# A fused attention and gated feed-forward kernel: the first block's output by seven products, and sums of the gates' weights on GpSimd

## The chip, the cores and the metric

The kernel runs on one core of a Trainium2 chip. The metric is the device time of one execution in microseconds (us). A core has a matmul engine (TensorE, PE in the profile; its weight loads are PEld), VectorE (DVE), ScalarE (ACT), GpSimd (POOL) and SyncE (SP). They run their own instruction streams and wait for each other by semaphores. Matmul results go to eight PSUM banks of 512 float32 a partition; here they are called pF0 to pF3 and pA0 to pA3.

## The reference

Attention with projected keys and values, then a gated feed-forward layer. There are 8 batches, 8 heads, a sequence of 1024 and a head size of 64; the projection has 64 rows.

```python
def _attn_ref(q, k, v, E, F):
    k_proj = np.einsum('ks,bhsd->bhkd', E, k)
    v_proj = np.einsum('ks,bhsd->bhkd', F, v)
    scale = 1.0 / np.sqrt(q.shape[-1])
    scores = scale * np.matmul(q, k_proj.transpose(0, 1, 3, 2))
    scores = scores - np.max(scores, axis=-1, keepdims=True)
    attn = np.exp(scores)
    attn = attn / (np.sum(attn, axis=-1, keepdims=True) + 1e-09)
    return np.matmul(attn, v_proj).astype(np.float32)

def _moe_ref(x, w_gate, w_val, w_out):        # x: 8192 x 512, d_ff 1536
    gate = 1.0 / (1.0 + np.exp(-(x @ w_gate)))
    val = x @ w_val
    return (gate * val @ w_out).astype(np.float32)
```

The output of attention, with the heads side by side, is `x`.

## The kernel before

The 8192 rows are worked on in 16 blocks of 512, two to a batch. For a block the kernel makes the gates and values (`x @ w_gate`, `x @ w_val`), their product `hT`, and the output `hT @ w_out`. Nearly everywhere a product of two matrices, each cut in 2 x 2 quarters, is made of seven products of quarters instead of eight (Strassen's scheme in Winograd's form). The price is sums of quarters, made beforehand: `xs_sums` of the inputs, `s_sums` of `hT`, and sums of the weights, which are made once: `vt_sums` (values, buffer vT), `gt_sums` (gates, buffer gT) and `t_sums` (output, buffer wT). Two exceptions stand at the start: the gates of blocks 0 and 1 and the values of block 0 are plain products, and so is the output of block 0:

```python
        def oproj(blk, tt, pb, cols=((0, DM),)):
            # ... o is a row of vsnap or ost
            for n, (c0, c1) in enumerate(cols):
                # ...
                for m in range(NF):                        # NF = 12
                    mm(pb, bank[pb][:, 0 : c1 - c0],
                       hT[blk % 2][:, m, tt * P : (tt + 1) * P],
                       wO[:, m, c0:c1], ...)               # 512 columns
                dve(lambda e, pb=pb, c0=c0, c1=c1: e.tensor_scalar(
                        o[:, c0:c1], bank[pb][:, 0 : c1 - c0], 0.5, None, op0=ALU.mult), ...)
                # ... the store of o
```

(Calls are joined to fewer lines in this section, and "..." marks cuts.) A block's output by seven products looks like this; `a` and `c` are two banks, and a product is twelve matmuls of 256 columns:

```python
        def o_chain(blk, a, c, goal, step, sums=True):
            # ...
            if sums:
                for n in (1, 2, 3):
                    s_sums(blk, n, (0, 6))
            prod(a, "A11", "B11", True)
            seed(a, c)                  # ACT copies bank a to bank c
            prod(c, "A12", "B21")
            evac(c, 0, 0)               # ACT, to the output buffer
            s_sums(blk, 4, (0, 6))
            prod(a, "S2", "T2")
            keep_snap(0, a)             # ACT, to a buffer in SBUF
            prod(a, "A21", "T3")
            keep_snap(1, a)
            prod(c, "S1", "T1", True)
            add_snap(1, c, 1, 1)        # DVE, bank c plus the kept one
            prod(a, "A22", "T4")
            evac(a, 1, 0)
            stored(blk, (2, 3))
            prod(c, "A12", "B22")
            add_snap(0, c, 0, 1)
            stored(blk, (0, 1))
```

The sums of the gates' weights; each writes a third or all of one buffer of gT (the one numbered 1 overwrites a part of `wG` itself), and VectorE makes all of them:

```python
        def gt_sums(n, part=None):
            c0, c1 = (0, DFF // 2) if part is None else (256 * part, 256 * part + 256)
            # ... B11 to B22: quarters of wG
            T = [gT[:, k, :, c0:c1] for k in range(3)]
            o, a, b, op = {
                3: (T[1], B22, B12, ALU.subtract),
                1: (B12, B12, B11, ALU.subtract),
                2: (T[0], T[1], B11, ALU.add),
                4: (T[2], B21, T[0], ALU.subtract),
            }[n]
            # ...
            dve(lambda e: e.tensor_tensor(o, a, b, op), r, w, t=0.95 if part is None else 0.42)
```

The first part of the program, up to block 0's output, stands in an order set by hand: `todo` is a list of slots of TensorE's work, and `put` or `on(u, j, ...)` hangs other work on a slot. After the plain gates of block 0 (slots 0 to 10) come three groups of pieces (`u` = 0, 1, 2), the quads K = 3, 4, 5 of block 1, with batch 1's attention among them. Then:

```python
        on(1, 6, lambda: (load_k(2), load_v(2), load_q(2)))       # issued from GpSimd's queue
        # ...
        on(2, 0, h_sums(1, A, 1))
        on(2, 4, h_sums(1, A, 2, 3))
        on(3, 0, h_sums(1, Z, 1, 2, 3))
        for tt in range(4):
            todo.append(lambda tt=tt: oproj(0, tt, FF.take()))
        on(3, 1, n1["outputs"])
        on(3, 2, lambda: n1["bc"](0))     # bc: attention's scaling, two rounds
        on(3, 3, lambda: n1["bc"](1))
```

All that follows is put in order by a list scheduler with times of its own (`arranged`), from `goal`, the wished start. Its first part is, before the change:

```python
        for n in (3, 2):
            t_sums(n)
        for n in (3, 2, 4):
            gt_sums(n)
        gt_sums(1)
        for n in (1, 2, 3, 4):
            xs_sums(2, n)
        next_kv(2, -2.0)                  # projects K and V of batch 2: 16 matmuls
        transpose_q(["kpB"])
        t_sums(4)
        t_sums(1)
        o_chain(1, OA, OC, 0.0, 2.0, sums=False)
        # ... then the chains of quads 6 to 47, with attention among them
```

Every engine takes its own instructions in the order of the program. All loads stand in GpSimd's queue; of those that matter here `second_loads` issues Q, K and V of batch 1 and the two halves of `wO`, the latter once Q of batch 1 has been transposed. The order of `load_w` at the start is that of the pieces of `wG` and `wV`, 256 columns each.

Of the kernel before, what the change touches and what calls it, by code (L numbers as in the profile page):

```python
# [7 lines left out]
ALU = mybir.AluOpType  # L8
# [229 lines left out]
def bass_linformer_attn__then__ffn_glu_sigmoid_kernel(  # L238
# [18 lines left out]
    with contextlib.ExitStack() as es:  # L257
# [33 lines left out]
        bsel8 = within([P, 4, 2, 64], BF16)  # L291
        kp = within([P, NR, DH], BF16)
        rhi = within([P, 256], BF16)
        rhl = within([P, 256], BF16)
        early[0], used[0] = gT[:, :, :, :].rearrange("p a b c -> p (a b c)"), 0
# [176 lines left out]
        def start_loads():  # L472
# [18 lines left out]
            load_w(0, 1)  # L491
            load_w(1)
            load_w(2)
            for R in range(2):
                load_q_half(0, 1, R)
            load_w(3)
            load_w(4)
            load_w(5)
# [456 lines left out]
        def attention(b):  # L955
# [90 lines left out]
            def bc(rnd):  # L1046
                bks = [AA.take() for _ in range(4)]
# [11 lines left out]
                for j in range(4):  # L1059
                    n = 4 * rnd + j  # L1060
                    mul(n // 2, n % 2, bks[j])
                    AA.append(bks[j])
# [230 lines left out]

        def gate(blk, m, pg, pv):
            M = blk * NF + m
# [18 lines left out]
        def oproj(blk, tt, pb, cols=((0, DM),)):  # L1314
            o = vsnap[tt][:, :] if tt < 2 else ost[:, tt, :]
            ok = [("vsnap", tt)] if tt < 2 else None
            t = 2 * (2 * (blk % 2) + tt % 2) + tt // 2
            for n, (c0, c1) in enumerate(cols):
                if n:
                    pb = FF.take()  # L1320
                for m in range(NF):
                    mm(
                        pb,
                        bank[pb][:, 0 : c1 - c0],
                        hT[blk % 2][:, m, tt * P : (tt + 1) * P],
                        wO[:, m, c0:c1],
                        [("hT", blk % 2, m, tt // 2)] + (["wO0", "wO12"] if m < H6 else ["wO1"]),
                        start=(m == 0),
                        stop=(m == NF - 1),
                    )  # L1330
                dve(
                    lambda e, pb=pb, c0=c0, c1=c1: e.tensor_scalar(
                        o[:, c0:c1], bank[pb][:, 0 : c1 - c0], 0.5, None, op0=ALU.mult
                    ),
                    [],
                    ok or [("ost", tt, x) for x in ((0, 1) if len(cols) == 1 else (n,))],
                    b=pb,
                )
                FF.append(pb)
                add(  # L1340
                    "SP",
                    lambda e, c0=c0, c1=c1: e.dma_start(out_v[blk // 2, t][:, c0:c1], o[:, c0:c1]),
                    r=ok or [("ost", tt, x) for x in ((0, 1) if len(cols) == 1 else (n,))],
                    dma=f"out{tt}" if n == 0 else "outlast",
                )

        H6 = NF // 2

        def t_sums(n):
# [6 lines left out]
                4: (T4, B21, T2, ALU.subtract, ["wO1", ("wT", 2)], [("wT", 4)]),  # L1360
                1: (B12, B12, B11, ALU.subtract, ["wO0"], ["wO12", ("wT", 1)]),
            }[n]
            if n == 4:
                w = w + ["bsel8", ("kp", 0), ("kp", 1)]
                w += [(k, R) for k in ("rhi", "rhl") for R in range(2)]
            dve(lambda e: e.tensor_tensor(o, a, b, op), r, w, t=0.95)

        def s_sums(blk, n, ms, eng="DVE"):
# [4 lines left out]
            S1, S2 = hS[:, 0, lo, :], hS[:, 1, lo, :]  # L1373
# [14 lines left out]
        def part(blk, x, up):  # L1388
            if x[0] == "S":
                return [(x, m) for m in up]  # L1390
            return [("hT", blk % 2, m + H6 * (x[2] == "2"), int(x[1]) - 1) for m in up]
# [200 lines left out]
        def gt_sums(n, part=None):  # L1592
# [15 lines left out]
            if n != 1:  # L1608
                w += ["rows", "ident"] + [("rden", c, R) for c in range(2) for R in range(2)]
# [518 lines left out]
```

The softmax here doesn't subtract the row's maximum and nothing guards it: scores larger than these inputs give would overflow.

## Time and profile before

| | |
|---|---|
| time, median of 3 runs | 517.52 us (517.07 to 517.91) |
| span of the profiled execution | 515.9 us |
| TensorE busy | 505.0 us (98%), clock 1.000 |
| VectorE busy | 410.9 us (80%) |
| ScalarE busy | 345.0 us (67%) |
| GpSimd busy | 41.0 us (8%) |
| moved by DMA | 63.13 MB, mean 122 GB/s |

The profile is of one execution. Busy time is the time in which an engine had an instruction at work; the ends of matmuls are modelled, so that a busy TensorE need not be at its peak. VectorE's busy share by stretches of 10 us is 8.0 of 10 us from 60 to 70, 8.8 from 70 to 80, 9.5 from 80 to 90 and 8.4 from 90 to 100; the last two hold the four sums of the gates' weights, 0.95 us each, and the four of the output's weights, 0.95 us each. A line of a timeline has start and time in us, the engine, the line of the kernel, the operation, what it writes and reads, the shape and how many of them; the brackets at the end tell how long the engine sat idle before and what ended it.

### The profile page before, as it was taken

What the parts mean: (1) busy time and instruction counts of PE and PEld (TensorE: products, weight loads), DVE (VectorE), ACT (ScalarE), POOL (GpSimd) and SP (SyncE); (2) the same over time, 40 slices, a digit from 0 to 9 for tenths busy, and PEclk for the clock granted to TensorE, in tenths of its full rate; (3) what the DMA queues carried; (4) which work ended last, traced back from release to release, by engine and by line L of the source; (5) the groups of instructions that cost most, each with busy time, mean ns of one, the idle gap of its engine ahead of it and who ended that gap; (6) DMA issues with size and microseconds to landing.
All of it is one profiled execution on the core that took longest, in us unless ns stands there. A gap on an engine that the chain in (4) does not pass through costs nothing.

```text
span 515.9 us, 11369 instructions
## 1 busy us (share of the span) xinstructions
PE 505.0 (98%) x4598; PEld 410.0 (79%) x4598; DVE 410.9 (80%) x809; ACT 345.0 (67%) x645; POOL 41.0 (8%) x60
## 2 busy tenths in 40 slices
PE   5999999999999999999999999999999999999996
PEld 3545645888888888888888888888888888888885
DVE  4548779899789796988879888797969898777774
ACT  2555683867778677677767776777676766676652
POOL 9420301200200020000100020000000000000000
PEclk9999999999999999999999999999999999999999
DMA  9999999899798788454946389374104330201013
GB/s 161 199 198 204 150 195 221 115 178 233 93 224 155 152 150 138 102 125 123 174 85 154 60 152 203 56 164 100 46 7 97 42 104 1 83 1 76 6 43 124
DMA packets 105205, 63.13 MB, mean 122 GB/s; under 512 B 63040, under 2 KB 97344, under 8 KB 105152
## 3 DMA queue, kind: packets, MB, share of 16 engines
q0 software_dynamic: 34000, 29.89, 37.5%
q1 hardware_dynamic: 71152, 32.52, 28.8%
q8 instruction: 36, 0.59, 0.4%
q14 instruction: 17, 0.14, 0.1%
HBM read 60.29 MB, written 16.78 MB: 149 GB/s over the span
## 4 chain that ended last, share of the span: by engine, by line
PE 94%; DMA 2%; DVE 1%; POOL 1%; issue 0%; ACT 0%; DVEq 0%; POOLq 0%
PE pA L385 51%; PE pF L385 43%; DMA KVs<-in_v_dram 2%; DVE hT L1832 0%; POOL KVs L403 0%; DVE vsnap L1710 0%; POOL Qb L403 0%; DVE xT L868 0%; DVE ost L1437 0%; ACT sig L389 0%; DVE sig L1786 0%; ACT vsnap L389 0%; DVE ost L1522 0%; POOL quad L482 0%; DVE hS L1382 0%
## 5 line engine op out<-in xcount | busy, mean ns | idle before, releaser
L389 ACT ACTIVATE sig<-pA 128x512 f32<-128x512 f32 x126 | 75.1, 596 | 43.4 <-PE pA L385 42.8
L1699 ACT ACTIVATE pF<-pA 128x512 f32<-128x512 f32 x99 | 58.5, 591 | 30.9 <-PE pA L385 26.3
L1710 DVE TENSOR_TENSOR vsnap<-pF,vsnap 128x512 f32<-128x512 f32 x90 | 61.8, 686 | 18.1 <-ACT vsnap L389 9.2
L1786 DVE TENSOR_TENSOR sig<-pF,sig 128x512 f32<-128x512 f32 x84 | 57.5, 685 | 7.2 <-PE pA L385 3.7
L385 PE MATMUL pF<-wO,hT 128*128 128x256 bf16 (+1 forms) x402 | 59.3, 285 | 0.0
L389 ACT ACTIVATE vsnap<-pA 128x512 f32<-128x512 f32 x84 | 50.2, 597 | 11.9 <-PE pA L385 11.8
L1832 DVE SCALAR_TENSOR_TENSOR hT<-sig,vsnap 128x512 bf16<-128x512 f32 x84 | 56.6, 683 | 0.9
L389 ACT ACTIVATE sig<-sig 128x512 f32<-128x512 f32 x84 | 52.8, 629 | 2.9 <-DVE sig L1786 2.6
L385 PE MATMUL pF<-xS,wV 128*128 128x256 bf16 x360 | 54.0, 273 | 0.1
L385 PE MATMUL pA<-xT,gT 128*128 128x256 bf16 x336 | 50.4, 273 | 0.0
L385 PE MATMUL pF<-xS,wG 128*128 128x256 bf16 x336 | 50.4, 273 | 0.0
L385 PE MATMUL pA<-xT,vT 128*128 128x256 bf16 x336 | 50.4, 273 | 0.0
L385 PE MATMUL pF<-xT,wG 128*128 128x256 bf16 (+1 forms) x264 | 50.2, 311 | 0.2 <-DVE xT L868 0.2
L389 ACT ACTIVATE sig<-pF 128x512 f32<-128x512 f32 x66 | 39.5, 598 | 15.0 <-PE pF L385 13.1
L385 PE MATMUL pA<-wT,hT 128*128 128x256 bf16 x360 | 48.8, 273 | 0.1
L1832 DVE SCALAR_TENSOR_TENSOR hT<-sig,pF 128x512 bf16<-128x512 f32 x42 | 28.7, 683 | 24.6 <-PE pF L385 24.4
L385 PEld LDWEIGHTS pF<-wO,hT 128*128 128x128 bf16 x402 | 38.7, 98 | 10.5 <-issue 0.8
L385 PE MATMUL pF<-xT,wV 128*128 128x256 bf16 (+1 forms) x240 | 41.5, 294 | 0.0
L385 PEld LDWEIGHTS pF<-xS,wV 128*128 128x128 bf16 x360 | 34.9, 98 | 6.1 <-DVE vsnap L1710 0.4
L385 PEld LDWEIGHTS pA<-wT,hT 128*128 128x128 bf16 x360 | 34.3, 98 | 5.6 <-ACT EF L389 0.8
L389 ACT ACTIVATE eT<-pA 128x512 bf16<-128x512 f32 x58 | 34.1, 596 | 5.7 <-PE pA L385 4.4
L385 PEld LDWEIGHTS pA<-xT,vT 128*128 128x128 bf16 x336 | 32.3, 98 | 5.2 <-issue 0.4
(159 smaller groups left out, 906.5 us busy)
## 6 DMA issues: line engine op xcount, KB each, us to landing
out_dram<-ost SPq DMA_DIRECT2D x61, 256.0 KB, 2.5
Qb<-in_q_dram POOLq DMA_DIRECT2D x7, 1024.0 KB, 11.9
KVs<-in_k_dram POOLq DMA_DIRECT2D x7, 1024.0 KB, 13.7
KVs<-in_v_dram POOLq DMA_DIRECT2D x7, 1024.0 KB, 18.0
wO<-in_moe_w_out_dram POOLq DMA_DIRECT2D x2, 768.0 KB, 9.8
wG<-in_moe_w_gate_dram POOLq DMA_DIRECT2D x5, 256.0 KB, 18.9
wV<-in_moe_w_val_dram POOLq DMA_DIRECT2D x5, 256.0 KB, 19.4
KVs<-in_k_dram POOLq DMA_DIRECT2D x2, 512.0 KB, 9.3
```

Of the source, the lines that this page charges most:

```text
L385: return add("PE", lambda e: e.matmul(o, lhsT, rhs, **kw), r=r, x=[("bank", b)])
L389: return add("ACT", lambda e: e.activation(o, i, func, scale=scale), r=r, w=w, x=x, t=t)
L1699: lambda e: e.activation(bank[c][:, :], bank[a][:, :], AF.Copy, scale=1.0),
L1710: lambda e: e.tensor_tensor(o, bank[bk][:, :], o, ALU.add),
L1786: dve(lambda e: e.tensor_tensor(o, bank[bk][:, :], o, ALU.add), [key], [key], b=bk)
L1832: lambda e: e.scalar_tensor_tensor(o, sg.rearrange("p (j c) -> p j c", j=2), 1.0, x.rearrange("p (j c) -> p j c", j=2), ALU.add, ALU.mult,),
```

## The change

The output of block 0 is made by seven products as well, in pieces set by hand (`o_pieces`) in the place of the four calls of `oproj`. This needs the sums of block 0's `hT` (`s_sums`), put into slots as the plain gates allow, which are made in another order for it; they have two borrowed buffers (`EF` and `xS[0]`). It also needs the output's weight sums earlier (`t_sums`, from the scheduled part to slots ahead of the products). To make room on VectorE, eleven of the twelve pieces of the gates' weight sums go to GpSimd, and one stays: nine of them are put ahead of the loads of batch 2 in GpSimd's queue, behind those of `wO`, a tenth after them and still ahead of the loads, the eleventh behind the loads. Buffers for constants move so that gT is free early. The second round of attention's scaling moves to the scheduled part, and the projection of batch 2 has a later goal. What is computed stays the same.

The diff, without the removed text of `oproj`:

```diff
--- before.py
+++ after.py
@@ -288,11 +288,10 @@
         identf = within([P, P], FP32)
         bsel8f = within([P, 4, 2, 64], FP32)
         early[0], used[0] = wT[:, :, :, :].rearrange("p a b c -> p (a b c)"), 0
-        bsel8 = within([P, 4, 2, 64], BF16)
         kp = within([P, NR, DH], BF16)
-        rhi = within([P, 256], BF16)
-        rhl = within([P, 256], BF16)
-        early[0], used[0] = gT[:, :, :, :].rearrange("p a b c -> p (a b c)"), 0
+        bsel8 = sbuf("bsel8", [P, 4, 2, 64], BF16)
+        rhi = sbuf("rhi", [P, 256], BF16)
+        rhl = sbuf("rhl", [P, 256], BF16)
         rden = within([P, 256], FP32)
         rows = within([P, 4, 32], FP32)
         ident = within([P, P], BF16)
@@ -489,12 +488,12 @@
                 load_kv_heads(1, v, R)
             load_w(0, 0)
             load_w(0, 1)
+            load_w(3)
             load_w(1)
-            load_w(2)
             for R in range(2):
                 load_q_half(0, 1, R)
-            load_w(3)
             load_w(4)
+            load_w(2)
             load_w(5)
 
         def heads8():
@@ -1043,8 +1042,19 @@
                     [("rhl", R) for R in range(2)],
                 )
 
-            def bc(rnd):
-                bks = [AA.take() for _ in range(4)]
+            def bc(rnd, goal=None, bks=None):
+                if goal is None:
+                    bks = [AA.take() for _ in range(4)]
+                    bc_mm(rnd, bks)
+                else:
+                    with group(goal, 0.5):
+                        bc_mm(rnd, bks)
+                for j in range(4):
+                    n = 4 * rnd + j
+                    mul(n // 2, n % 2, bks[j])
+                    AA.append(bks[j])
+
+            def bc_mm(rnd, bks):
                 for half_ in range(2):
                     for j in range(4):
                         jj = slice(32 * j, 32 * j + 32)
@@ -1056,10 +1066,6 @@
                             ["bsel8", ("rhl", j // 2)],
                             tp=(32 * j, 0),
                         )
-                for j in range(4):
-                    n = 4 * rnd + j
-                    mul(n // 2, n % 2, bks[j])
-                    AA.append(bks[j])
 
             def xo_one(r, bks):
                 for g in range(2):
@@ -1291,8 +1297,11 @@
                 stop=(i == NI - 1),
             )
 
+        turns = [0]
+
         def gate(blk, m, pg, pv):
-            M = blk * NF + m
+            M = turns[0]
+            turns[0] += 1
             sg = sig[M % 3]
             act(
                 sg, bank[pg][:, :], [], [("sig", M % 3, 0)], b=pg, func=AF.Tanh, scale=0.5
@@ -1311,43 +1320,6 @@
                 b=pv,
             )
 
-        def oproj(blk, tt, pb, cols=((0, DM),)):
... (its removed lines)
         H6 = NF // 2
 
         def t_sums(n):
@@ -1357,20 +1329,28 @@
             o, a, b, op, r, w = {
                 3: (T3, B22, B12, ALU.subtract, ["wO1", "wO12"], [("wT", 3)]),
                 2: (T2, T3, B11, ALU.add, ["wO0", ("wT", 3)], [("wT", 2)]),
-                4: (T4, B21, T2, ALU.subtract, ["wO1", ("wT", 2)], [("wT", 4)]),
+                4: (T4, B21, T2, ALU.subtract, ["wO1", ("wT", 2), ("rhl", 0)], [("wT", 4)]),
                 1: (B12, B12, B11, ALU.subtract, ["wO0"], ["wO12", ("wT", 1)]),
             }[n]
             if n == 4:
-                w = w + ["bsel8", ("kp", 0), ("kp", 1)]
-                w += [(k, R) for k in ("rhi", "rhl") for R in range(2)]
+                w = w + [("kp", 0), ("kp", 1), "rows", "ident"]
+                w += [("rden", c, R) for c in range(2) for R in range(2)]
             dve(lambda e: e.tensor_tensor(o, a, b, op), r, w, t=0.95)
+
+        def S_of(blk):
+            if blk:
+                return [hS[:, x, :, :] for x in range(2)]
+            return [
+                EF[:, 0:768].bitcast(BF16).rearrange("p (m c) -> p m c", c=256),
+                xS[0][:, :, :, :].rearrange("p a i c -> p (a i) c"),
+            ]
 
         def s_sums(blk, n, ms, eng="DVE"):
             h, (m0, m1) = hT[blk % 2], ms
             lo, hi, up = slice(m0, m1), slice(H6 + m0, H6 + m1), range(m0, m1)
             A11, A21 = h[:, lo, 0:256], h[:, lo, 256:512]
             A12, A22 = h[:, hi, 0:256], h[:, hi, 256:512]
-            S1, S2 = hS[:, 0, lo, :], hS[:, 1, lo, :]
+            S1, S2 = (x[:, lo, :] for x in S_of(blk))
             o, a, b, op, r, w = {
                 1: (S1, A21, A22, ALU.add, "A21 A22", "S1"),
                 2: (S2, S1, A11, ALU.subtract, "S1 A11", "S2"),
@@ -1387,6 +1367,11 @@
 
         def part(blk, x, up):
             if x[0] == "S":
+                if blk == 0:
+                    return [
+                        [("EF", "E"), ("EF", "F"), ("snap", 0), ("snap", 1)],
+                        [("xS", 0, k) for k in (1, 2, 4)],
+                    ][int(x[1]) - 1] + [(x + "z", m) for m in up]
                 return [(x, m) for m in up]
             return [("hT", blk % 2, m + H6 * (x[2] == "2"), int(x[1]) - 1) for m in up]
 
@@ -1395,7 +1380,7 @@
             for j in js:
                 for m in range(*ms):
                     if A[0] == "S":
-                        lhsT = hS[:, int(A[1]) - 1, m, j * P : (j + 1) * P]
+                        lhsT = S_of(blk)[int(A[1]) - 1][:, m, j * P : (j + 1) * P]
                     else:
                         c = 256 * (A[1] == "2") + j * P
                         lhsT = h[:, m + H6 * (A[2] == "2"), c : c + P]
@@ -1463,6 +1448,26 @@
         def evac(bk, tok, col):
             o, keys = quarter(tok, col)
             act(o, bank[bk][:, :].rearrange("p (j c) -> p j c", j=2), [], keys, b=bk, scale=0.5)
+
+        def o_pieces(blk):
+            a, c = FF.two()
+
+            def p(*x):
+                return lambda: product(blk, *x)
+
+            def do(*fns):
+                return lambda: [fn() for fn in fns]
+
+            return [
+                do(p(a, "A11", "B11", True), lambda: seed(a, c)),
+                do(p(c, "A12", "B21"), lambda: evac(c, 0, 0)),
+                do(p(a, "S2", "T2"), lambda: keep_snap(0, a)),
+                p(c, "S1", "T1", True),
+                do(p(a, "A21", "T3"), lambda: keep_snap(1, a), lambda: add_snap(1, c, 1, 1)),
+                do(p(a, "A22", "T4"), lambda: evac(a, 1, 0), lambda: stored(blk, (2, 3))),
+                do(p(c, "A12", "B22"), lambda: add_snap(0, c, 0, 1), lambda: stored(blk, (0, 1))),
+                lambda: (FF.append(a), FF.append(c)),
+            ]
 
         def o_chain(blk, a, c, goal, step, sums=True):
             turn = [0]
@@ -1589,7 +1594,7 @@
             op = ALU.add if n == 2 else ALU.subtract
             dve(lambda e: e.tensor_tensor(o, a, b, op), r, w)
 
-        def gt_sums(n, part=None):
+        def gt_sums(n, part=None, gp=False):
             c0, c1 = (0, DFF // 2) if part is None else (256 * part, 256 * part + 256)
             js = (0, 1, 2) if part is None else (part,)
             B11 = wG[:, 0:2, c0:c1]
@@ -1605,14 +1610,15 @@
             }[n]
             r = [("wG", j + k, x) for j in js for k in (0, 3) for x in range(2)]
             w = [("gT", n, j) for j in js]
-            if n != 1:
-                w += ["rows", "ident"] + [("rden", c, R) for c in range(2) for R in range(2)]
             if n == 1:
                 r, w = [("wG", j, 0) for j in js], w + [("wG", 3 + j, 0) for j in js]
             if n == 2:
                 r = [("wG", j, 0) for j in js] + [("gT", 3, j) for j in js]
             if n == 4:
                 r = [("wG", j, 1) for j in js] + [("gT", 2, j) for j in js]
+            if gp:
+                pool(lambda e: e.tensor_tensor(o, a, b, op), r, w)
+                return
             dve(
                 lambda e: e.tensor_tensor(o, a, b, op), r, w, t=0.95 if part is None else 0.42
             )
@@ -1937,14 +1943,14 @@
 
         A, Z = (0, 4), (4, 6)
         todo.append(lambda: first_pair(0, lambda: xo(1)))
-        for m in range(2, NF):
+        for m in (6, 7, 2, 3, 8, 9, 4, 5, 10, 11):
             todo.append(lambda m=m: mstep(0, m))
         qt2, sc2, den2, bc2, xo2 = half_unit(1, att)
         put(3, lambda: (qt2(0, ("DVE", "ACT")), qt2(1, ("DVE", "ACT"))))
         put(4, lambda: (sc2(0), sc2(1)))
         put(4, second_loads)
         put(6, lambda: (den2(), xo2(0), xo2(1)))
-        put(7, lambda: (vt_sums(3, 0), vt_sums(2, 0)))
+        put(6, lambda: (vt_sums(3, 0), vt_sums(2, 0)))
         put(8, lambda: bc2(0)())
         put(9, lambda: bc2(1)())
         put(10, x_sums(1, 1, 2))
@@ -2002,12 +2008,21 @@
                 on(u, 0, lambda: [late1(x, g) for x in ("A0", "A1") for g in range(2)])
         on(2, 0, h_sums(1, A, 1))
         on(2, 4, h_sums(1, A, 2, 3))
-        on(3, 0, h_sums(1, Z, 1, 2, 3))
-        for tt in range(4):
-            todo.append(lambda tt=tt: oproj(0, tt, FF.take()))
+        o0 = []
+        on(2, 8, lambda: (o0.extend(o_pieces(0)), o0[0]()))
+        todo.extend([lambda n=n: o0[n]() for n in (1, 3, 2, 4, 5, 6, 7)])
+        on(3, 0, lambda: [t_sums(n) for n in (3, 1, 2)])
         on(3, 1, n1["outputs"])
-        on(3, 2, lambda: n1["bc"](0))
-        on(3, 3, lambda: n1["bc"](1))
+        on(3, 1, lambda: t_sums(4))
+        on(3, 3, h_sums(0, (0, 6), 4))
+        on(3, 4, lambda: n1["bc"](0))
+        for i in range(9):
+            put(6 + i // 2, lambda i=i: gt_sums((3, 2, 4)[i % 3], i // 3, True))
+        put(3, h_sums(0, (0, 2), 1, 2))
+        put(4, h_sums(0, (0, 2), 3))
+        on(1, 8, h_sums(0, (2, 6), 1, 2, 3))
+        on(1, 1, lambda: gt_sums(1, 0, True))
+        on(2, 1, lambda: gt_sums(1, 1, True))
 
         for i, slot in enumerate(todo):
             slot()
@@ -2023,6 +2038,7 @@
         def when(K):
             return PACE * (K - 6)
 
+        n1["bc"](1, 0.5, (GA, OA, VA, XB))
         blocks_ready(1)
         blocks_ready(2)
 
@@ -2033,17 +2049,13 @@
             vd_one(XA, 0, b % 2)
             vd_one(XA, 1, b % 2, b > 3)
 
-        for n in (3, 2):
-            t_sums(n)
-        for n in (3, 2, 4):
-            gt_sums(n)
-        gt_sums(1)
+        for n in (1, 2, 3):
+            s_sums(1, n, Z)
+        gt_sums(1, 2)
         for n in (1, 2, 3, 4):
             xs_sums(2, n)
-        next_kv(2, -2.0)
+        next_kv(2, 3.0)
         transpose_q(["kpB"])
-        t_sums(4)
-        t_sums(1)
         o_chain(1, OA, OC, 0.0, 2.0, sums=False)
         for n in (1, 2, 3, 4):
             xs_sums(3, n)
```

More of the change, by code (lines that the diff above doesn't have):

```diff
@@ L1312, in gate @@
             )
-        def oproj(blk, tt, pb, cols=((0, DM),)):
[L1315 to L1345, printed above, removed]
         H6 = NF // 2
```

## The prediction

> **What bounds the kernel now.** I read the page's busy table and its slices first, then the chain that ended last, then the timeline of single engines in the stretch that the change touches (56 to 100 us).
>
> The page:
>
> ```profile
> span 515.9 us, 11369 instructions
> PE 505.0 (98%) x4598; PEld 410.0 (79%) x4598; DVE 410.9 (80%) x809; ACT 345.0 (67%) x645; POOL 41.0 (8%) x60
> ...
> PE 94%; DMA 2%; DVE 1%; POOL 1%; issue 0%; ACT 0%; DVEq 0%; POOLq 0%
> ```
>
> TensorE is 94% of the chain. "Busy" alone would not prove it full, since ends of matmuls are modelled, so I took the distance from start to start: the chain has stretches such as "2.62 PE pA L385 x24", 0.109 us for a matmul of 256 columns, and between 100 and 500 us nearly all neighbours stand at that distance. Only less matmul work, or fewer waits of TensorE, can shorten the run; DVE time counts only where TensorE waits for it.
>
> The timeline of TensorE where block 0's output is made:
>
> ```profile
> 70.74 2.76 PE L385 MATMUL pF<-wO,hT 128*128 128x512 bf16 x12
> 73.44 0.62 PE L385 MATMUL pA<-eT,dsel 128*32 128x256 bf16 x16
> 73.99 0.41 PE L385 MATMUL pF<-eT,vpD 64*64 64x512 bf16 x4
> 74.23 0.39 PE L385 MATMUL pA<-eT,vpD 64*64 64x512 bf16 x4
> 74.55 2.76 PE L385 MATMUL pF<-wO,hT 128*128 128x512 bf16 x12
> 77.24 0.40 PE L385 MATMUL pA<-wT 32*128 32x256 bf16 x8
> 77.57 2.76 PE L385 MATMUL pF<-wO,hT 128*128 128x512 bf16 x12
> 80.27 0.60 PE L385 MATMUL pA<-wT 32*128 32x256 bf16 x8
> 80.80 2.76 PE L385 MATMUL pF<-wO,hT 128*128 128x512 bf16 x12
> ```
>
> Columns are start, time, engine, line, operation. These are the four output tiles of twelve matmuls, with attention between them and no real gap. At 83.50 sixteen matmuls follow that project K and V of batch 2. The timeline of GpSimd in that stretch:
>
> ```profile
> 58.44 1.65 POOL L403 DMA_DIRECT2D wO<-in_moe_w_out_dram  x2 [23.35 <-DMA qT<-Qb]
> 60.06 0.91 POOL L403 DMA_DIRECT2D KVs<-in_k_dram  x1
> 60.93 0.92 POOL L403 DMA_DIRECT2D KVs<-in_v_dram  x1
> 61.80 0.92 POOL L403 DMA_DIRECT2D Qb<-in_q_dram  x1
> 83.56 0.97 POOL L917 MEMSET xu<- 128x1040 bf16 x1 [20.84 <-issue]
> ```
>
> GpSimd does little, but its queue issues the loads, in order. Of the issues between 56 and 90 us:
>
> ```profile
> KVs<-in_k_dram POOLq DMA_DIRECT2D x1, 1024.0 KB, 15.6
> KVs<-in_v_dram POOLq DMA_DIRECT2D x1, 1024.0 KB, 21.3
> ```
>
> So V of batch 2 lands at 60.93 + 21.3 = 82.2 us, and TensorE uses it at 83.50: 1.3 us to spare. This is the number that decides.
>
> **What the Trainium skill says.** "GPSIMD Engine Reference", § 3.1 Elementwise: a two-input tensor_tensor takes GpSimd some 2.6 cycles an element, 4497 ns for 2048 float32 a partition. A quarter of it, for the 512 elements of each sum here, is 1.12 us: an estimate from that page; the trace before has no GpSimd arithmetic to compare, only a memset of 128x1040 at 0.97 us.
>
> The same page, § 2.1 Instruction dispatch: the first call into a freshly loaded library of GpSimd routines pays about 6 us more. The built program of the changed kernel has a library load ahead of GpSimd's first sum, and the kernel before has none. No run here shows its cost yet.
>
> "SBUF — State Buffer", § Who interferes with whom: a VectorE instruction with two SBUF inputs and a GpSimd instruction that reads SBUF exclude each other, the later one waiting. The trace before cannot show it.
>
> **The change, part by part.**
>
> 1. Products. Removed: 48 matmuls of 512 columns, 4 x 2.70 us start to start = 10.8. Added: 7 products of 12 matmuls of 256 columns, 84 x 0.109 = 9.2. Gain 1.6 us at most, and all on the path if nothing waits.
>
> 2. What the seven products wait for. They use only two banks and copies between them. ACT, after the late exponentials, has one seed copy (0.59) more ahead of the four xu copies, which end at 73.4 now; then the first evacuation. Hence the product S1 T1, which starts its bank anew, waits some 0.5 to 0.9 us. S2 T2 is followed directly by A21 T3 in the same bank, and between them ACT must copy the bank: 0.6 us and the hand-over, 0.7 us. A22 T4 waits 0.3 us likewise, as the eight small matmuls between are shorter than the copy. Sum 1.5 to 1.9 us. Parts 1 and 2 cancel: TensorE reaches batch 2's projection at 83 to 84 us as now.
>
> 3. VectorE. Out: four sums of gates' weights at 0.95 us = 3.8 (one piece of 0.42 stays), four evacuations at 0.69 = 2.8. In: block 0's own sums, 3 x 0.42 + 3 x 0.68 + 0.95 = 4.3, and two additions at 0.69 = 1.4. Some 0.5 us less in total, but the load moves out of 84 to 96 us into earlier slots. Of TensorE's waits behind 83.5 us I find 0.16 us at 88.3, 0.2 at 91.1 and some of 0.09: 0.5 us could go.
>
> 4. Weight loads in another order, and gates 6, 7 ahead of 2, 3: the same bytes at the same places in the queue, each still ahead of its use. Zero.
>
> 5. GpSimd's queue. Nine sums stand behind the two loads of wO, a tenth after them, and only then K, V and Q of batch 2. The first sum cannot start before 60.1 us (wO's issue waits for a transpose of Q that the change leaves alone). Ten sums of 1.1 to 1.3 us, with the exclusion and the waits of one for another, are 11 to 13 us; the library load adds nothing to 6 us. K is thus issued at 71 to 73 us without the load's cost, at 77 to 79 with it, against 60.06.
>
> From K's issue to V's landing: at 98.25 us, with no queue in front, K took 10.2 us and V, issued 0.86 later, 16.7: 17.6 together. Between 60 and 82 us wO landed at 59.25 + 11.3 = 70.6 and V 11.6 after. [...]I take 14 to 17 us. V then lands at 86 to 89 us, or at 92 to 95.
>
> In the changed program these sixteen matmuls still come directly after the second round of attention's scaling, ahead of all of block 1's output, and TensorE takes its instructions in order. It stands still from 83.5 to the landing: 2.5 to 5.5 us, or 8.5 to 11.5. Nothing behind makes this good, since TensorE is full there. DVE delays in the stretch before hide inside this wait.
>
> Sum: -1.6 (products) +1.7 (their waits) -0.5 (later gaps) +2.5 to 5.5 or +8.5 to 11.5: some +3.5 us or +9.5 us. I choose 523.5, +6.0, between them, nearer neither: I know too little of the library load to put all on one.
>
> **The rivals.**
>
> First, products win. If GpSimd does a bf16 sum in about 0.5 us and the library costs nothing, K is issued at 65 us, V still streams behind wO and lands before 83.5. Then only parts 1 to 3 count: -0.5 to -2 us, 515.5 to 517. For it: the change puts these sums on an engine that the page shows 8% busy, and it lets batch 2's projection have a later goal. Against it: the size of the page's figure.
>
> Second, VectorE is the new bound. T3, T1 and T2 (0.95 us each) come directly ahead of the products that need them; if each loses a turn to a GpSimd sum of 1.1 us, three to five us are added to a VectorE that is 88% busy from 70 to 80 us, and S1 T1, S2 T2 and the scaling come late. Alone that makes +2 to +4 us, 520 to 521.5; together with a late V it is mostly hidden.
>
> Third, the late transfers of batch 2 cost more than V's wait: Q comes after V, its four transposes with it, and the heads need them some 12 us after the projection. Now the first head starts 9.3 us after that projection, so I expect no wait; if there is one, 2 to 4 us more, 527 to 530.
>
> **Range and chances.** The low end is the first rival's upper edge, 517; the high end is a full library load with slow sums, 530. Faster by 2% would need 507.2, far more than the 1.6 us the products can bring: 0.01. Slower by 2% is 527.9, a V landing after some 94 us, possible with the library load at its full cost: 0.27. The rest, 0.72, is within 2%.
>
> **What would show it right or wrong.** In the changed profile: GpSimd's timeline with the sums' duration and the start of the first; K's issue after 70 us; TensorE's idle time ahead of the matmuls that read KVs, put down to the load of V; a distance of block 0's output to the one before that differs little. Wrong would be: V landed before TensorE is there, or TensorE waiting longer for VectorE's sums than for V.

## The result, and the profile after

The changed kernel takes 529.23 us (median; 528.65 to 531.09), the kernel before 517.43 us on the same chip. The ratio is 1.0233, with a 95% interval from 1.0212 to 1.0253: 2.3% slower.

The page of the changed kernel:

```profile
span 526.9 us, 11459 instructions
PE 506.5 (96%) x4634; PEld 414.5 (79%) x4634; DVE 416.7 (79%) x811; ACT 349.7 (66%) x650; POOL 56.9 (11%) x71
PEclk9999979999999999999999999999999999999999
PE 89%; DMA 4%; DVE 3%; ACT 2%; POOL 1%; issue 1%; DVEq 0%; ACTq 0%; POOLq 0%
```

TensorE's share of the chain fell from 94% to 89%: it waits more. And its clock, a 9 in all forty slices before (1.000 over the span), has one slice of 7. The profile is that of the fastest of the five executions.

GpSimd's timeline, where the prediction put the whole loss:

```profile
57.97 1.65 POOL L402 DMA_DIRECT2D wO<-in_moe_w_out_dram  x2 [23.19 <-DMA qT<-Qb]
59.69 1.18 POOL L1620 TENSOR_TENSOR gT<-wG 128x512 bf16<-128x512 bf16 x1
...
62.19 1.65 POOL L1620 TENSOR_TENSOR gT<-wG,gT 128x512 bf16<-128x512 bf16 x1
...
73.15 1.60 POOL L1620 TENSOR_TENSOR wG<-wG 128x512 bf16<-128x512 bf16 x1
74.69 0.93 POOL L402 DMA_DIRECT2D KVs<-in_k_dram  x1
75.62 0.89 POOL L402 DMA_DIRECT2D KVs<-in_v_dram  x1
```

The first sum starts 0.07 us after the issue of wO ends (57.97 + 1.65), so no library load shows in front of it; where it was made is not in the trace. A sum takes 1.16 to 1.18 us alone, and 1.48 to 1.65 from the third on. Ten of them hold the queue for 15.0 us. Of the DMA issues in this stretch (the last number is us from issue to landing):

```profile
KVs<-in_v_dram POOLq DMA_DIRECT2D x1, 1024.0 KB, 14.0
```

So V lands at 75.62 + 14.0 = 89.6 us, against 82.2 before. Now TensorE's timeline:

```profile
63.87 1.03 PE L384 MATMUL pF<-xT,wG 128*128 128x512 bf16 x4
68.77 1.03 PE L384 MATMUL pF<-xT,wV 128*128 128x256 bf16 x4 [3.87 <-ACT pF L1705]
69.59 1.06 PE L384 MATMUL pF<-xS,vT 128*128 128x256 bf16 x4
...
77.93 0.41 PE L384 MATMUL pF<-qT,kpD 64*64 64x512 bf16 x3 [0.45 <-DVE vsnap L1716]
...
81.01 0.62 PE L384 MATMUL pA<-eT,dsel 128*32 128x256 bf16 x16 [0.82 <-ACT xu L388]
...
85.60 1.48 PE L384 MATMUL pF<-wT,hT 128*128 128x256 bf16 x12 [0.69 <-ACT EF L388]
...
87.86 1.47 PE L384 MATMUL pF<-wT,hT 128*128 128x256 bf16 x12 [0.45 <-ACT EF L388]
...
91.20 1.92 PE L384 MATMUL pA<-KVs,EFT 128*64 128x512 bf16 x16
```

The last line is the projection of batch 2, at 91.20 us instead of 83.50, with no wait in brackets: V had been there for 1.6 us. TensorE lost its time before. The 3.87 us wait ahead of 68.77 is put down to a copy by ScalarE, but that copy waited for VectorE. ScalarE's line, and VectorE's timeline in the same stretch:

```profile
68.13 0.58 ACT L1705 ACTIVATE pF<-pF 128x512 f32<-128x512 f32 x1 [3.89 <-DVE vsnap L1716]
```

```profile
62.74 1.65 DVE L1362 TENSOR_TENSOR EF<-hT 128x1024 bf16<-128x1024 bf16 x1
64.42 1.52 DVE L1362 TENSOR_TENSOR xS<-EF,hT 128x1024 bf16<-128x1024 bf16 x1
65.86 1.63 DVE L1362 TENSOR_TENSOR hT<-hT 128x1024 bf16<-128x1024 bf16 x1
67.42 0.68 DVE L1716 TENSOR_TENSOR vsnap<-pF,vsnap 128x512 f32<-128x512 f32 x1
```

Block 0's three sums, predicted at 0.68 us each, take 1.5 to 1.65, turn about with GpSimd's. The addition behind them (L1716), one of whose inputs is in PSUM, takes its usual 0.68; ScalarE's copy waits for it, and TensorE for the copy. Next, after that wait, four matmuls of 256 columns take 1.03 us instead of 0.60. Busy time by stretch (the last columns are granted clock, DMA share and GB/s):

```profile
68.70:74.00 5.30, 5.23 (x21) 3.14 (x22) 5.04 (x5) 2.69 (x6) 5.14 (x4) 0.50 0.06 9
```

TensorE ran at half clock for 5.3 us (the trace has the half clock from 67.2 to 74.0), while the DMA engines, waiting for GpSimd to issue, moved next to nothing. The kernel before has 1.00 in the same stretch. Last, TensorE's timeline some 85 us later, and what stands behind the wait in the queues of GpSimd and SyncE:

```profile
154.32 0.39 PE L384 MATMUL pA<-qT,xu 128*128 128x512 bf16 x1 [3.15 <-DMA xu<-kpd]
```

```profile
142.46 0.88 POOL L402 DMA_DIRECT2D KVs<-in_v_dram  x1 [33.53 <-PE pA L384]
155.07 0.88 POOL L402 DMA_DIRECT2D KVs<-in_k_dram  x1 [11.73 <-DMA xu<-kpd]
```

```profile
143.41 1.36 SPq L936 DMA_TRANSPOSE xu<-kpd  x1
```

The load of a later batch's V is issued 1.0 us ahead of the transpose that the next heads need, and the transpose takes 10.9 us to land. In the kernel before, the transpose came first and landed in 5.0 us:

```profile
131.50 1.29 SPq L937 DMA_TRANSPOSE xu<-kpd  x1
```

```profile
137.75 0.88 POOL L403 DMA_DIRECT2D KVs<-in_k_dram  x1 [36.88 <-PE pA L385]
138.62 0.89 POOL L403 DMA_DIRECT2D KVs<-in_v_dram  x1
```

### The profile page after: what moved, and what is told of

Read it like the earlier page. It is cut to its first block, busy times and chain, and to the rows that moved or that the text cites. A ratio compares the mean times of both kernels' runs of the same rounds, so it can differ in the third digit from the quotient of the medians.

```text
span 526.9 us, 11459 instructions
## 1 busy us (share of the span) xinstructions
PE 506.5 (96%) x4634; PEld 414.5 (79%) x4634; DVE 416.7 (79%) x811; ACT 349.7 (66%) x650; POOL 56.9 (11%) x71
## 4 chain that ended last, share of the span: by engine, by line
PE 89%; DMA 4%; DVE 3%; ACT 2%; POOL 1%; issue 1%; DVEq 0%; ACTq 0%; POOLq 0%
PE pA L384 48%; PE pF L384 41%; DMA KVs<-in_v_dram 2%; DMA xu<-kpd 2%; DVE vsnap L1716 1%; ACT xu L388 1%; DVE hT L1838 0%; ACT pF L1705 0%; POOL KVs L402 0%; DVE EF L1362 0%; ACT EF L388 0%; DVE hT L1362 0%; DVE xS L1362 0%; POOL Qb L402 0%; ACT kpd L388 0%
## 5 line engine op out<-in xcount | busy, mean ns | idle before, releaser
L1716 DVE TENSOR_TENSOR vsnap<-pF,vsnap 128x512 f32<-128x512 f32 x90 | 61.8, 687 | 20.0 <-PE pF L384 9.6
L384 PE MATMUL pF<-wO,hT 128*128 128x256 bf16 x390 | 52.7, 273 | 0.0
L384 PEld LDWEIGHTS pF<-xS,wG 128*128 128x128 bf16 x336 | 32.2, 98 | 5.3 <-issue 1.2
```

The source lines that it names most:

```text
L384: return add("PE", lambda e: e.matmul(o, lhsT, rhs, **kw), r=r, x=[("bank", b)])
L1716: lambda e: e.tensor_tensor(o, bank[bk][:, :], o, ALU.add),
```

## The experiments

The theory after the result, A: GpSimd's sums cost through three things that are not V's landing (the exclusion with VectorE's sums of two SBUF inputs, the half clock that comes with the long wait, the turned order of loads at 142 us). Rivals: B, the late loads of batch 2 are the cost after all; C, the seven products cost the time with their own waits. All ratios are to the kernel before.

**The products alone.** All sums of the gates' weights back on VectorE:

```diff
-            put(6 + i // 2, lambda i=i: gt_sums((3, 2, 4)[i % 3], i // 3, True))   # in a loop of nine; the loop goes too
-        on(1, 1, lambda: gt_sums(1, 0, True))
-        on(2, 1, lambda: gt_sums(1, 1, True))
-        gt_sums(1, 2)
+        for n in (3, 2, 4):
+            gt_sums(n)
+        gt_sums(1)
```

> The changed kernel with all sums of the gates' weights back on VectorE, in the scheduled part as before; the seven products of block 0 stay. Theory A (GpSimd's sums and VectorE's two-input sums exclude each other, TensorE waits 3.9 us for a bank that VectorE releases late and then runs 5 us at half clock): the three sums of block 0 at 62 us take 0.69 us each, no half clock, V of batch 2 lands at about 82 us; 516.5 to 519 us, or 3 us more if the transpose of batch 4's K still stands behind V's load (the 3.2 us wait at 151 us). Theory B (V's late load is what costs): the same time, but no difference in VectorE's durations. Theory C (the seven products cost it themselves): 525 us or more.

520.76 us, ratio 1.0069 [1.0050, 1.0089]. C holds in part: +3.5 us without GpSimd's sums, of which 2.6 us are there by batch 2's projection (86.07 against 83.50). The wait that took 3.87 us is now

```profile
66.18 0.61 PE L384 MATMUL pF<-xT,wV 128*128 128x256 bf16 x4 [1.12 <-ACT pF L1705]
```

with VectorE's sums at 0.68 to 0.69 us, and there is no half clock and no wait near 150 us. The order of the later loads is turned here too (V at 138.67, K at 142.34), so that is not GpSimd's doing alone. But the transpose, at 138.00, stands behind two transposes of Q instead of three and goes out 0.67 us ahead of V; it lands in 3.5 us.

**GpSimd's sums alone**, on the kernel before with its plain output (the constants' buffers moved as in the change).

```diff
+        # the nine, one and one sums on GpSimd at the slots of the change
-        for n in (3, 2, 4):
-            gt_sums(n)
-        gt_sums(1)
+        gt_sums(1, 2)
```

> The kernel before with only the sums of the gates' weights moved to GpSimd; block 0's output by plain products as before. Theory A: block 1's sums (0.69 us alone) at 64 to 68 us take some 1.6 us and VectorE comes 3 to 5 us late, but what stands behind them is less urgent; 519 to 522 us. Theory B: V lands at 89 to 90 us and TensorE, at 83.5 us, waits 5 to 6 us for it: 522 to 524 us, with a wait of TensorE put down to KVs. Theory C: 517 to 518 us.

528.32 us, ratio 1.0214 [1.0195, 1.0233]. TensorE's timeline:

```profile
85.71 0.40 PE L384 MATMUL pA<-KVs,EFT 128*64 128x512 bf16 x1
92.26 3.54 PE L384 MATMUL pA<-KVs,EFT 128*64 128x512 bf16 x15 [6.15 <-DMA KVs<-in_v_dram]
```

The wait that the prediction described, in size between its two cases (up to 5.5, from 8.5 us): V issued at 75.37, landed 16.8 later at 92.2, TensorE ready at 85.7. The clock halves within the wait, at 88.8, and stays so until 95.6, so that the fifteen matmuls take 3.54 us. The expected 522 to 524 us lacked that (1.7 us), and waits for VectorE by which TensorE was ready 2.2 us later than before the change. B is true of this kernel for the larger part.

**VectorE's colliding sums moved behind the fifth quad.**

```diff
-        on(1, 8, h_sums(0, (2, 6), 1, 2, 3))
+        on(3, 0, h_sums(0, (2, 6), 1, 2, 3))      # ahead of t_sums
```

> The changed kernel with the three sums of block 0's second part put behind quad 5's VectorE work instead of ahead of the addition that releases quad 4's bank. Theory A: the wait of 3.9 us at 65 us and the half clock go (6.5 us); then V's landing at 89 to 90 us becomes the wait that ends last and takes some 3 to 5 us of it back; 523 to 526 us. If nothing hides behind (theory A alone, V never late): 521 to 523 us. Theory B: 528 us as the changed kernel.

530.79 us, ratio 1.0258 [1.0230, 1.0287]. The wait at 65 us is gone; in its place attention's scores wait 1.7 us at 70 for an addition that stands behind a VectorE instruction of two SBUF inputs (1.67 us), and the product S1 T1 waits 3.3 us at 76 for T1, which takes 1.90 us itself and stands behind block 0's sums (1.64, 1.53 and 0.68 us). 6.8 us of half clock begin in that wait. The collision moved along with the sums; the projection came at 90.88. At 151 us TensorE waits 4.0 us for the transpose, with 6.8 us more of half clock. The time is over every one that I expected.

**GpSimd writes zeros instead of reading weights.** This leaves out the sums of the gates' weights on GpSimd: memsets of 128x1536, some 1.4 us each, stand in their place, so the gates are not the reference's.

```diff
-                pool(lambda e: e.tensor_tensor(o, a, b, op), r, w)
+                pool(lambda e: e.memset(gT[:, k, :, :], 0.0), r, w + extra)
```

> The changed kernel with GpSimd writing zeros into the buffers of the gates' sums, 1536 elements a partition, in place of the sums of 512: the same number of instructions at about 1.4 us each that write SBUF but read nothing. It leaves out ten of GpSimd's sums and the eleventh, so the gates are not the reference's. Theory A as the Trainium skill has it (the exclusion is against GpSimd instructions that read SBUF): VectorE's sums take 0.69 us, no wait at 65 us, no half clock, V lands at about 88 us; 522 to 525 us. If any busy GpSimd holds VectorE back: 528 us and sums of 1.6 us as in the changed kernel.

528.64 us, ratio 1.0225 [1.0194, 1.0256]. GpSimd's and TensorE's timelines:

```profile
58.82 14.16 POOL L1622 MEMSET gT<- 128x1536 bf16 x10
```

```profile
64.95 0.61 PE L384 MATMUL pF<-xT,wV 128*128 128x256 bf16 x4 [1.12 <-ACT pF L1707]
...
87.63 3.48 PE L384 MATMUL pA<-KVs,EFT 128*64 128x512 bf16 x15 [2.38 <-DMA KVs<-in_v_dram]
```

The queue is held as long (14.16 us), but VectorE's sums are back at 0.68 to 0.69 us and the wait at 65 us at 1.12. So it is GpSimd's reading, not its being busy, that holds VectorE's sums back. This is what the Trainium skill says in "SBUF — State Buffer", § Who interferes with whom: a VectorE instruction with two SBUF inputs contends with a GpSimd instruction that reads SBUF, not with one that only writes it. What was won came straight back: TensorE reaches the projection at 84.84 and waits for V, which the exclusion had hidden, with 3.4 us of half clock. The wait near 150 us grew to 5.1 us, with 6.8 us of half clock, so the time did not fall clear of the noise (the runs go from 526.98 to 530.62 us).

**Batch 2's loads ahead of the sums.**

```diff
-            put(6 + i // 2, lambda i=i: gt_sums((3, 2, 4)[i % 3], i // 3, True))
+            on(1, 7, lambda i=i: gt_sums((3, 2, 4)[i % 3], i // 3, True))
-        on(1, 1, lambda: gt_sums(1, 0, True))
+        on(1, 7, lambda: gt_sums(1, 0, True))
```

> The changed kernel with the loads of K, V and Q of batch 2 ahead of all ten sums in GpSimd's queue; the sums start some 2.7 us later and so still run beside VectorE's two-input sums. If the late V is what costs the time: V lands near 82 us as before the change, and the time falls by the 6 us that the run with GpSimd's sums alone waited for V, to 521 to 523 us. If the exclusion between GpSimd and VectorE and the half clock behind the first wait are what costs it: V lands early and nobody notices, batch 2's projection still starts at 88 to 91 us with VectorE's sums of 128x1024 at 1.5 us and more, and the time stays at 526 to 529 us.

530.53 us, ratio 1.0266 [1.0237, 1.0295]. V landed at 60.06 + 19.5 = 79.6, ten microseconds earlier, and the projection still came at 91.19. The sums, now later, still met block 0's (1.64, 1.52 and 1.63 us), and the wait at 65 us was 4.8 us. With the exclusion in place, V's landing is worth nothing; B is false of the changed kernel. The wait near 150 us stayed (3.2 us), now with 3.4 us of half clock.

**V's later loads behind the transpose.**

```diff
-                load_v(b, done)
+                load_v(b, done + ["kpB"])
```

> The changed kernel with one list of dependences longer: V's later loads stand behind the transpose of K's projection, as they stood before the change. If the 3.2 us wait at 151 us comes from that load standing ahead of the transpose: the wait goes, nothing else changes, 525.5 to 526.5 us. If the wait is only TensorE being early after its delay, it turns up elsewhere: 528 to 529.5 us.

525.06 us, ratio 1.0158 [1.0141, 1.0175]. The wait of 3.15 us is gone, and the transpose, again issued at 143.4, lands in 3.1 us instead of 10.9. V is now issued at 147.36, once the transpose has landed. The time fell a little further than the wait (by 0.0075 in the ratio, some 3.9 us), as this profile has 3.4 us of half clock and the changed kernel's 6.8.

**Nine sums where GpSimd only waits** (between the loads of batch 1 and those of wO), the last two behind the loads.

```diff
             transpose_q()
+            for i in range(9):
+                gt_sums((3, 2, 4)[i % 3], i // 3, True)
             for x, w in enumerate((["wO0", "wO12"], ["wO1"])):
-            # the loop of nine at slots 6 to 10
-        on(1, 1, lambda: gt_sums(1, 0, True))
+        on(1, 7, lambda: gt_sums(1, 0, True))
```

> The changed kernel with nine of GpSimd's ten sums moved ahead of the loads of wO, into the 23 us in which its queue only waits for a transpose of Q (35 to 58 us), and the tenth behind the loads of batch 2. VectorE's, ScalarE's and TensorE's instructions are the same and in the same order. If GpSimd's place in time is the cause of both the late V and the exclusion: V lands at 82 to 83 us, VectorE's sums of block 0 are back at 0.69 us, no half clock near 67 us, and the time is that of the run with all sums on VectorE or a little less: 517.5 to 521 us. If the seven products themselves, or the library of GpSimd routines, cost the time: it stays over 524 us.

528.54 us, ratio 1.0217 [1.0194, 1.0240]: far over what I expected. V landed at 80.3 and there was no half clock near 67, but two causes were left. The tenth and eleventh sums, at 62.1 to 64.9, hit exactly block 0's first sum (1.64 us), and TensorE waited 2.8 us; and the wait near 150 us stayed, 3.2 us with 3.4 us of half clock behind it: V is issued 1.0 us ahead of the transpose here too (139.10 and 140.11).

**Both causes out of the way**: the edit above and that of V's load, and the other pieces on VectorE in one sum (`gt_sums(1)` in the scheduled part).

> The changed kernel with three edits at once: nine sums on GpSimd ahead of the loads of wO, the three pieces left on VectorE as one sum in the scheduled part, and V's later loads behind the transpose of K's projection. So GpSimd does nothing between 62 and 90 us. If GpSimd's place in its queue and the turned order of loads are the whole of what it costs: the wait at 65 us is back at 1.3 us, no half clock, no wait at 150 us, and the time is that of the run with all sums on VectorE less its two waits for these sums at 93 us (1.2 us): 519 to 520 us. If GpSimd's sums cost something by themselves: 522 us or more.

520.43 us, ratio 1.0054 [1.0034, 1.0075]. TensorE's timeline:

```profile
65.59 0.61 PE L384 MATMUL pF<-xT,wV 128*128 128x256 bf16 x4 [1.13 <-ACT pF L1705]
```

No half clock, no wait near 150, the projection at 85.48. The ratio falls by 0.018, some 9 us, with the same nine sums on GpSimd. What is left (1.0054) is no more than in the run with all sums on VectorE (1.0069): the seven products and what came with them.

**The products' own waits.** First block 0's sums five slots earlier, into idle time of VectorE, with all gates' sums on VectorE:

```diff
-        on(1, 8, h_sums(0, (2, 6), 1, 2, 3))
+        on(1, 3, h_sums(0, (2, 6), 1, 2, 3))
```

> The run with all sums of the gates' weights back on VectorE, and with block 0's three sums of 128x1024 moved five slots earlier, into VectorE's idle time from 57.7 to 60.2 us. If these three sums ahead of an addition are what makes TensorE wait 1.3 us at 64.7 us: that wait goes, and the time falls from 520.8 to 519.3 to 519.8 us. If the wait is the seed's own on ScalarE: it stays, 520.5 to 521 us.

520.10 us, ratio 1.0057 [1.0042, 1.0072]. The wait at 64.7 us went. The time differs from the run with unmoved sums by less than the intervals tell apart (the profiled span by 1.6 us). Then the products themselves rearranged:

```diff
-                p(c, "S1", "T1", True),
+                lambda: (d.append(FF.take()), p(d[0], "S1", "T1", True)(), FF.append(c)),   # d also in the last product
-        on(3, 1, n1["outputs"])
-        on(3, 1, lambda: t_sums(4))
-        on(3, 4, lambda: n1["bc"](0))
+        on(3, 0, lambda: t_sums(4))       # rden, rows, ident lie in gT
+        on(3, 3, n1["outputs"])
+        on(3, 5, lambda: n1["bc"](0))
```

with six of GpSimd's sums early (in this run and the next two, V's later loads stand behind the transpose):

> Against the waits inside the seven products: S1 T1 in a third bank, attention's output matmuls behind S2 T2 in the place of its wait for the copy of its bank, T4 made without waiting for attention's scaling (its constants moved), block 0's three sums five slots earlier. Six of GpSimd's sums ahead of wO, the others on VectorE, V's later loads behind the transpose. If the rest of the loss is the waits of the seven products (1.0 + 0.85 us and the 1.3 us at 65 us): 515.5 to 517.5 us, level with the kernel before or just under it. If the waits only move to the next product: 518 to 520 us.

and with all on VectorE:

> The same rearranged products with all sums of the gates' weights on VectorE. If GpSimd, once out of the way, is worth what VectorE's sums cost TensorE at 93 us: 1 to 1.5 us above the run with the third bank and GpSimd's early sums, so 516.5 to 518.8 us. If it is worth nothing: the same time within 0.3 us.

520.66 us, ratio 1.0046 [1.0031, 1.0062], and 521.19 us, 1.0065 [1.0046, 1.0084]. The waits of 0.99 and 0.85 us and that at 65 us went as meant, and others came behind, as the less favourable expectation had it: 1.3 us ahead of A22 T4 for a copy, and 1.7 us in three pieces in the second round of scaling, which waits for VectorE's multiplications. Whether the sums are better on GpSimd or VectorE stays open here, as the intervals overlap. Last, batch 2's projection put ahead of that round to fill the 1.7 us (its goal -30 instead of 3):

> The run with the third bank and GpSimd's early sums, with the projection of batch 2 ahead of the second round of attention's scaling, which waited 1.7 us in three pieces for VectorE's multiplications of the first round. If these waits are only a matter of what TensorE has to do meanwhile: the projection (1.9 us) fills them, 1.5 to 1.7 us off, to 0.1% above the kernel before, 517.5 to 519 us. If what follows the second round becomes late instead (the third batch's inputs, then its quads): no gain, 520 to 521 us.

521.02 us, ratio 1.0061 [1.0047, 1.0074]. The fill worked (projection at 83.51), and the round's late multiplications became a 1.95 us wait of the next quad (1.79 us of it idle), with 3.4 us of half clock behind it. No version beats the kernel before.

## Where the prediction was right and where wrong, step by step

Predicted were 523.5 us (+6.0), with a chance of 0.27 on slower by over 2%. The time, 529.23 (+11.8), lies at the upper end of the range of 517 to 530, and that is luck: V's landing, on which the range was built, cost nothing. Both of the prediction's own signs of being wrong came true: V landed (89.6) before TensorE was there (91.20), and TensorE waited longer for VectorE's sums (3.87 us, by way of ScalarE's copy) than for V (no wait).

The span grew by 11.0 us (515.9 to 526.9). From the timelines:

| | us |
|---|---|
| the products' fewer matmuls | -1.6 |
| waits among the products (0.63, 0.99, 0.85, 0.61) | +3.1 |
| wait at 65 us: 1.28 as with the sums on VectorE | +1.3 |
| the same wait, by the exclusion: 4.03 - 1.28 | +2.75 |
| half clock: from the end of that wait to block 0's first product (68.77 to 75.24) 6.47 us; with the sums on VectorE 3.92 | +2.55 |
| all before 60 us | -0.3 |
| projection of batch 2: 91.20 - 83.50 | 7.7 |
| wait for the transpose at 151 us, small rest | +3.3 |

(The waits of this table, and those given above without a line, are taken from start to start, less the distance at which matmuls follow each other unhindered; they are some 0.17 us longer than in the brackets.) From block 0's first product to the projection it is 15.96 us in the changed kernel and 15.97 with the sums on VectorE: V cost nothing.

1. *Products, 1.6 us.* Right: a product takes 1.31 us from start to start where nothing waits, seven 9.2 us.

2. *Their waits, 1.5 to 1.9 us.* Right in kind for three, too small in size: 0.99, 0.85 and 0.61 us against 0.5 to 0.9, 0.7 and 0.3. The first stood one step ahead of S1 T1, before attention's sums of exponentials, which wait for ScalarE's copies. Missed were 0.63 us, in which attention's scores wait for VectorE's addition, and 1.3 us at 65 us, where block 0's sums stand ahead of the addition that frees a bank. "Parts 1 and 2 cancel" was wrong by 2.8 us; the products alone are slower.

3. *VectorE, -0.5 us.* About right where it was looked for: TensorE's waits from 90 to 100 us are 1.3 us with the gates' sums on VectorE and 0.1 with them early on GpSimd; 0.3 before the change. What was wrong is that the load could move into "earlier slots" for nothing: block 0's sums there are the 1.3 us of point 2.

4. *Weight loads, zero.* Right: batch 1's projections stand 0.3 us earlier than before.

5. *GpSimd's queue.* Of the terms, a sum alone was well sized (1.16 to 1.18 us against 1.12 worked out from the Trainium skill, "GPSIMD Engine Reference", § 3.1 Elementwise); ten took 15.0 us, not 11 to 13, through the exclusion; no library load showed ahead of the first sum, where up to 6 us were allowed for; K was issued at 74.69 and V landed at 89.6, between the two cases given. The step that failed is the conclusion: "It stands still from 83.5 to the landing" and "DVE delays in the stretch before hide inside this wait". It is the other way round: TensorE came to the projection at 91.20, 7.7 us late, because of those delays, the half clock and the products' own waits, and V's lateness hid in them. The runs with memsets and with the loads first show both sides: take the exclusion away and the wait for V appears; bring V early and nothing changes.

The second rival was nearest. It named the loss of turns between VectorE and GpSimd but looked at T3, T1 and T2, where the collision came with block 0's own sums. Its size, 2 to 4 us, fits the 2.75 us that the exclusion added to the wait; it lacked what a wait of that length does to TensorE's clock (2.55 us), and it held the delay to be hidden by V's, not the other way round. The third rival asked for late transfers of batch 2; what came late was the transpose of a later batch, through an order of loads that the rearranged list turned. The prediction did not look at the order behind the first projection, and the change had turned it.

What stays open: no run takes the half clock away without the wait, so its 2.55 us are read from the timeline. How much of it a wait brings varied between 0 and 6.8 us; where the wait falls explains that (last section), but the place was not set in any run.

## What to carry to other kernels

Work moved to an idle engine is not free of the busy one: see first whether both read SBUF at the same moment, the busy one with two inputs, and what stands behind the moved work in that engine's queue. A delay found in a queue costs only what is left when the consumer arrives, so work out both arrival times before adding waits up. The same nine sums cost nothing visible where GpSimd only waited and nothing of VectorE's with two inputs was urgent.

## What the runs showed of the hardware

- The exclusion is felt on both sides. VectorE's 128x1024 bf16 sum of two SBUF inputs took 0.68 to 0.69 us alone and 1.52 to 1.65 for block 0 in the changed kernel (1.04 once, where it met the end of a sum of GpSimd's); GpSimd's 128x512 sum went from 1.16 to between 1.48 and 1.65. VectorE's additions with one input in PSUM stayed at 0.68 to 0.69.
- TensorE's clock changed in steps of one length. In all fourteen profiles every stretch between two changes of the clock is a multiple of 3.413 us (3.41, 6.83, 58.03 = 17 x 3.413, 505.17 = 148 x 3.413), so that each trace can be cut into such windows. What TensorE's idle time in a window brought (ends of matmuls are modelled, so the idle times are rough):

| kernel | window, us | idle in it, us | clock in it | clock in the next |
|---|---|---|---|---|
| changed | 63.77 to 67.18 | 2.28 | full | half |
| changed | 67.18 to 70.59 | 1.59 | half | half |
| changed | 70.59 to 74.01 | 0.00 | half | full |
| changed | 149.10 to 152.51 | 1.34 | full | full |
| changed | 152.51 to 155.93 | 1.80 | full | full |
| nine sums early | 66.16 to 69.57 | 1.84 | full | full |
| projection first | 84.92 to 88.34 | 1.79 | full | half |

From 15 us to the last matmul of each profile, all ten windows of full clock with 2.2 us or more of idle time were followed by half clock, and none with less, but for the last line. Half clock went on behind the five windows of half clock with 0.98 us or more of idle time and ended behind the eleven with 0.54 or less. At half clock, matmuls of 256 columns follow at 213 instead of 109 ns. This is why the wait of 3.15 us at 151 us cost no clock: a border of windows cut it in two. "TensorE: Matmul & The Clock Gate" of the Trainium skill, Part 1, gives a free-running window of 3413 ns and half clock after an idle one; the length agrees with these traces, but some two thirds of a window were enough here (2.2 of 3.41 us).
- A DMA transpose took 10.9 us from issue to landing with a load of 1024 KB issued 1.0 us ahead of it; 7.5 with the load 0.03 us behind it (GpSimd's sums alone), 3.5 with it 0.67 us behind (all sums on VectorE), and 3.1 with it held back until the transpose had landed.
